# Windowed attention with a gated feed-forward: row maxima and the normalized x turned by VectorE in 32x32 blocks instead of by TensorE

## The chip, the cores and the metric

The kernel runs on one core of a Trainium2 chip. The metric is the device time of one execution in microseconds, the median of the runs. A core has five engines that run side by side: TensorE (PE, with its weight loads as PEld), VectorE (DVE), ScalarE (ACT), GpSimd (POOL) and SyncE (SP, which issues most DMAs).

## What is computed

x is 2048 rows of 512 numbers in float32. Cut to what matters:

```
xn = layernorm(x)                                  # over the 512 columns
q, k, v = split(xn @ wqkv)                         # 32 heads of 16
p = softmax(mask(q @ k.T / 4))                     # a row sees itself and the 255 rows before it
s = (p @ v) @ wo
f = (silu(xn @ w_gate) * (xn @ w_up)) @ w_down     # 1792 hidden columns
out = x + s * silu(f)
```

## The kernel before

**Numbers in two parts.** The large products run on TensorE in a reduced float32 format; every operand is split into a high part (`xh`, `wh`, `hh`) and the difference that is left (`xl`, `wl`, `hl`), and three products are added. The copy of the high part is made by ScalarE, the difference mostly by GpSimd, some of it by VectorE.

**Two halves.** The 128 rows of TensorE's array are used as two halves of 64 (`half(0)`, `half(1)`), each with a queue of matmuls of its own. A result is summed by half 0 first and then by half 1 in the same bank of PSUM; between the two stands a small VectorE copy of one column of that bank (`handover`, L608, tile `ho`), for which half 1 waits.

**Stages.** The 2048 rows are four chunks of 512. For each chunk `load_x` (L252) loads four tiles `xt` of 128 rows, takes mean and variance (VectorE) and scales the tiles (VectorE and GpSimd). `xt_turn` (L621) turns x so that its columns lie on the partitions: for each of four blocks `k` of 128 columns, eight TensorE transposes of 64x64 (four in each half) into two PSUM banks `xp`, then a ScalarE copy to `xh` and a VectorE difference to `xl`. Chunk 0 has a path of its own for the values (`x_turn`, L444), and goes through `xt_turn` as well. The turned x feeds the projections `a` (q and k), `vp` (v), `g` and `u` (gate and up); `d` is the down product and `s` the product with `wo`.

**Attention units.** There are 32 units, eight per chunk, of four heads each. `max_pair` (L1327) computes scores `b` of 128 queries and up to 384 keys; `ttr` (L1345) on VectorE adds the mask and takes the row maximum into a column of the tile `m` (16 columns a unit, one per head and block of queries). When all 16 are there, `max_turn` (L1368) turns `m` by TensorE: a transpose in half 0 into a bank `mt`, a handover copy by VectorE, a transpose in half 1, then a negating copy by ScalarE (`ms`) and a DMA of 8 KB (`put`) that lays the negated maxima as one more row under q. The scores are then computed again as `c`, this time with that row, so that the exponential on ScalarE (`p`) needs no further subtraction; GpSimd cuts the masked corners, and `pv_visit` (L1508) multiplies with the values, in both halves together.

**What sets the order.** A planner in the kernel writes all queues while the program is built. It keeps a clock for each half of TensorE and a queue for VectorE, ScalarE, GpSimd and the DMAs (`do`, L119; `dma`, L128), with a planned cost for each step. The dense matmuls form one long list; the attention steps (`streams`) and the loads (`marks`) have due times in units of 17.6 us of dense work (`PACE`), shifted by `LEAD`. A DMA counts as landed 3.5 us (`LAND`) plus `GUARD` after its issue. At run time every engine takes its instructions in the planned order and waits on semaphores for what it needs.

Of the kernel before, what the change touches and what calls it, by code (L numbers as in the profile page):

```python
# [17 lines left out]
P = 128  # L18
# [29 lines left out]
LAG = 7  # L48
MW = 80
SURE = 0.3  # L50
VDUE = 0.75


# [1 line left out]
PRIO = -0.5  # L55
MM = 0.2315
PACE = 17.6
LEAD = 1.12
OUT = 2.4
STEP = 0.05  # L60
LAND = 3.5
GUARD = 1.5


@with_exitstack
def tile_window_attention_swiglu_gate(
# [128 lines left out]

    ident = pers.tile([P, P], F32, name="ident")
    maskb = pers.tile([P, 3 * P], F32, name="maskb")
    mts = [pers.tile([P, MW], F32, name=f"m{i}") for i in range(2)]
# [11 lines left out]
    def constants2():  # L210
        one = take("one")
        nc.gpsimd.memset(one, 1.0)
        nc.gpsimd.memset(maskb, 0.0)
        nc.gpsimd.affine_select(
            maskb, maskb, [[-1, 3 * P]], ALU.is_ge, NEG, base=2 * P, channel_multiplier=1
        )
        nc.gpsimd.affine_select(
            maskb, maskb, [[1, 3 * P]], ALU.is_gt, NEG, base=0, channel_multiplier=-1
        )
        for t in mts:  # L220
            nc.gpsimd.memset(t, 0.0)
# [12 lines left out]
        nc.gpsimd.memset(vt[:, :, : H * VW].rearrange("p t (h c) -> p t h c", c=VW)[:, :, :, DH], 1.0)  # L234
        nc.gpsimd.memset(vt[:, :, H * VW :], 1.0)
# [16 lines left out]
    def load_x(c):  # L252
# [273 lines left out]
    def w_fetch(j):  # L526
# [18 lines left out]
        for n, (r, u) in enumerate(parts):  # L545
            last = n == len(parts) - 1
            dma(now[0], lambda r=r, u=u, last=last: go(r, u, last),
                lambda t, last=last: w_split(j, t, box[0]) if last else None,
                slack=1.0, can=lambda: box or rfree)

    def w_split(j, t, raw):
        w = [weighted[i].shape[1] if i in weighted else 0 for i in (j, j - 1)]
# [68 lines left out]
    def xt_turn(c, k):  # L621
        left = [2]
        for r in range(2):
# [28 lines left out]

            for t in range(4):
                extra[r].append((128, lambda t=t, go=go: go(t), finished if t == 3 else None))

    PAIRS = ((0, 0), (0, 1), (1, 0))

# [640 lines left out]
    def load_qk(u):  # L1298
# [17 lines left out]

        def then(t, n):
            if n == len(parts) - 1:
                qk_at[u] = t + 1.0
# [7 lines left out]
    def max_pair(u, p, qb):  # L1327
# [6 lines left out]
        for h in range(2):  # L1334
# [24 lines left out]
    mtp = {}  # L1359

    def turn_ready(u, r):
        if r == 0:
            if len(ttr_at.get(u, [])) < 16:
                return None
            return latest([max(ttr_at[u]) + 0.4, bank_time(rb_free)])
        return mtp[u][2]

    def max_turn(u, r):  # L1368
        if r == 0:
            mtp[u] = [*bank(rb_free, f"mt{u}"), None]  # L1370
        pb, tag, _ = mtp[u]

        def go():
            nc.tensor.matmul(
                pb[:MW, R * r : R * r + R], mts[u % 2][half(r), :], ident[half(r), half(r)],
                is_transpose=True, start=True, stop=True,
            )

        if r == 0:
            def after(t):  # L1380
                mtp[u][2] = t

            extra[0].append((128, go, lambda t: do("V", t, 0.09, lambda: handover(pb), after, -1.0)))
            return
        box = []

        def neg():
            box.append(sb(f"ms{u}", [16, P], F32R, "ms", 2))
            nc.scalar.activation(box[0], pb[:16, :P], AF.Copy, scale=-1.0)

        def after_neg(t):
            rb_free[tag] = t
            dma(t, put, lambda t: ms_at.__setitem__(u, t), -3.0, 8)

        def put():
            move(qs[u % 3][48 : 113 : 64], box[0])

        extra[1].append((128, go, lambda t: do("S", t, 0.25, neg, after_neg, -1.0)))

# [199 lines left out]
    def plan_attention():  # L1599
        for u in range(NU):  # L1600
# [2 lines left out]
                marks.append((u - 1 + 0.3, load_qk, (u,)))  # L1603
            for n in range(8):
                streams[0].append((u + 0.02 + 0.1 * n, max_ready, max_pair, (u, n // 4, n % 4)))
            streams[0].append((u + 0.8, turn_ready, max_turn, (u, 0)))
            streams[0].append((u + 0.8, turn_ready, max_turn, (u, 1)))
            ne = 3
            for n in range(2 * ne):
                streams[1].append((u + 1.07 + 0.13 * n, prob_ready, prob_pair, (u, n // 2, n % 2)))  # L1610
# [269 lines left out]
```

## Time and profile before

| | us |
|---|---|
| median of 3 runs | 849.04 (848.96 to 849.66) |
| the profiled execution | 856.25 |
| its span, first to last instruction | 854.5 |
| busy: PE / PEld | 846.9 / 759.8 |
| busy: DVE / ACT / POOL | 503.0 / 489.5 / 627.8 |

The granted TensorE clock is 0.991 of full speed over the span. A row of a group reads: line, engine, operation, output tile <- inputs, shapes, count | busy us, mean ns of one | idle us of the engine just before them, and what ended most of it. A row of waits reads: who waited, for whom, total us, times, longest. A row of the timeline reads: start us, length us, engine, line, operation, and in brackets the idle time before it.

### The profile page before, as it was taken

Reading aid. Unit: us, or ns where it says so; the run is one execution under the profiler, and the core shown is the slowest. Engines: PE = TensorE matmul, PEld = TensorE weight load, DVE = VectorE, ACT = ScalarE, POOL = GpSimd, SP = SyncE. Lnnn points to the kernel's source line nnn. Section 1 sums busy time; section 2 is a strip of 40 time slices with the busy share of each in tenths; the row PEclk is TensorE's granted clock in tenths of the full one; section 3 lists DMA queues with packets and bytes.
Section 4 is the critical chain, followed back from the end, with each engine's and each line's share of the span. In section 5 each row is a group of like instructions: output and inputs, shape, how many; then the busy total and the mean of one; then the engine's idle time right before and its main releaser. Section 6 shows DMA issues by size and latency. Waiting matters only on the chain.

```text
span 854.5 us, 26324 instructions
## 1 busy us (share of the span) xinstructions
PE 846.9 (99%) x10026; PEld 759.8 (89%) x10026; DVE 503.0 (59%) x1676; ACT 489.5 (57%) x950; POOL 627.8 (73%) x887
## 2 busy tenths in 40 slices
PE   8999999999999999999999999999999999999997
PEld 7999988888888989999889888888898899888987
DVE  5238476656666575666657666665646675554235
ACT  5543755556666456565666556656566665565531
POOL 5465877679768598668887687767687976888761
PEclk7999999999999999999999999999999999999999
DMA  5477865767776894578776876674877478754351
GB/s 141 125 203 165 223 151 151 175 155 179 153 191 159 228 226 112 127 197 163 182 164 141 239 187 178 142 183 118 195 184 199 117 169 206 178 136 122 101 140 51
DMA packets 67143, 139.98 MB, mean 164 GB/s; under 512 B 14710, under 2 KB 17654, under 8 KB 67016
## 3 DMA queue, kind: packets, MB, share of 16 engines
q1 hardware_dynamic: 66552, 137.64, 66.3%
q8 instruction: 79, 1.29, 0.7%
q10 hardware_dynamic: 464, 0.66, 0.3%
q14 instruction: 48, 0.39, 0.2%
HBM read 107.68 MB, written 29.62 MB: 161 GB/s over the span
## 4 chain that ended last, share of the span: by engine, by line
PE 98%; DMA 1%; DVE 0%; issue 0%; ACTq 0%; DVEq 0%
PE u L612 19%; PE d L612 19%; PE g L612 19%; PE a L612 11%; PE pv L1536 8%; PE vp L612 6%; PE c L1488 6%; PE s L612 5%; PE b L1340 4%; PE xp L632 1%; DMA xt<-x 1%; PE xp L450 0%; DVE xt L352 0%; DVE s L1189 0%; DVE st L347 0%
## 5 line engine op out<-in xcount | busy, mean ns | idle before, releaser
L572 POOL TENSOR_TENSOR wl<-wr,wh 128x512 fp32r<-128x512 f32 (+1 forms) x239 | 304.8, 1288 | 79.5 <-ACT wh L567 70.9
L1348 DVE CUSTOM_DVE_ANT_0 jk<-b,maskb 128x384 bf16<-128x384 f32 (+2 forms) x512 | 271.4, 530 | 91.2 <-PE b L1340 44.8
L1448 ACT ACTIVATE p<-c 128x512 f32<-128x512 f32 (+2 forms) x384 | 196.2, 573 | 61.7 <-PE c L1488 60.0
L612 PE MATMUL d<-wh,hh 64*128 64x512 f32 x896 | 227.6, 393 | 0.0
L567 ACT ACTIVATE wh<-wr 128x512 fp32r<-128x512 f32 (+1 forms) x239 | 145.8, 629 | 48.0 <-PE s L612 11.6
L612 PE MATMUL g<-xh,wl 64*128 64x512 f32 x448 | 161.3, 394 | 0.0
L612 PE MATMUL u<-xh,wh 64*128 64x512 f32 x448 | 160.8, 393 | 0.0
L612 PE MATMUL g<-xl,wh 64*128 64x512 f32 x448 | 160.6, 394 | 0.0
L612 PE MATMUL g<-xh,wh 64*128 64x512 f32 x448 | 160.3, 393 | 0.0
L612 PE MATMUL u<-xl,wh 64*128 64x512 f32 x448 | 160.2, 394 | 0.0
L612 PE MATMUL u<-xh,wl 64*128 64x512 f32 x448 | 159.8, 393 | 0.0
L612 PE MATMUL d<-wl,hh 64*128 64x512 f32 x448 | 152.7, 394 | 0.0
L612 PEld LDWEIGHTS d<-wh,hh 64*128 64x128 f32 x896 | 140.5, 185 | 6.7
L1460 POOL TENSOR_SCALAR_AFFINE_SELECT p<-p 128x256 f32<-128x256 f32 x256 | 101.6, 409 | 32.1 <-ACT p L1448 30.9
L767 POOL TENSOR_TENSOR hh<-h,hh 128x512 fp32r<-128x512 f32 x56 | 72.5, 1295 | 57.5 <-ACT hh L763 50.6
L1340 PE MATMUL b<-k,q 48*128 48x384 f32 (+2 forms) x512 | 110.6, 331 | 0.0
L1464 POOL TENSOR_SCALAR_AFFINE_SELECT p<-p 128x256 f32<-128x256 f32 x224 | 91.2, 410 | 15.6 <-ACT p L1448 14.1
L1488 PE MATMUL c<-q,k 49*128 49x128 f32 (+2 forms) x704 | 97.6, 299 | 0.0
L612 PE MATMUL a<-xl,wh 64*128 64x512 f32 x256 | 92.9, 392 | 0.0
L612 PE MATMUL a<-xh,wl 64*128 64x512 f32 x256 | 92.7, 392 | 0.0
L612 PE MATMUL a<-xh,wh 64*128 64x512 f32 x256 | 92.3, 392 | 0.0
L1488 PEld LDWEIGHTS c<-q,k 49*128 49x128 f32 x704 | 84.8, 186 | 6.5 <-DVE m L1348 1.1
(118 smaller groups left out, 1903.6 us busy)
## 6 DMA issues: line engine op xcount, KB each, us to landing
wr<-wgu SPq DMA_DIRECT2D x112, 256.0 KB
wr<-wdn SPq DMA_DIRECT2D x48, 256.0 KB
k<-qkd SPq DMA_DIRECT2D x48, 192.0 KB
wr<-wqk SPq DMA_DIRECT2D x32, 256.0 KB
qkd<-qkh SPq DMA_DIRECT2D x32, 256.0 KB
qkd<-qkl SPq DMA_DIRECT2D x32, 256.0 KB
q<-qkd SPq DMA_DIRECT2D x64, 128.0 KB
od<-ev SPq DMA_DIRECT2D x32, 256.0 KB
```

The source lines that it names most:

```text
L567: nc.scalar.activation(wtile[j, h][0][pr, a - 512 * h : b - 512 * h], raw[pr, a:b], AF.Copy)
L572: nc.gpsimd.tensor_tensor(lo, raw[pr, a:b], f32(hi), op=ALU.subtract)
L612: return nc.tensor.matmul(pb, a, b, start=first, stop=last, skip_group_check=True)
L632: nc.tensor.matmul(pb[:, R * t : R * t + R], xt[c, t][half(r), k * P : (k + 1) * P], ident[half(r), half(r)], is_transpose=True, start=Tru ...
L767: nc.gpsimd.tensor_tensor(hl[:, 1, :], self.h, f32(hl[:, 0, :]), op=ALU.subtract)
L1340: nc.tensor.matmul(pb[:, :n], qs[u % 3][r : r + 48, p, qb * P : (qb + 1) * P], ks[u % 3][r : r + 48, p, lo : lo + n], start=True, stop=True,)
L1348: nc.vector.tensor_tensor_reduce(junk[:, :n], pb[:, :n], maskb[:, 3 * P - n :], 1.0, -3.0e38, ALU.add, ALU.max, m[:, col : col + 1],)
L1448: nc.scalar.activation(t[:, h, :], pc[:, :n], AF.Exp, scale=DH ** -0.5)
L1460: nc.gpsimd.affine_select(s, s, [[0, 2], [1, P]], ALU.is_ge, 0.0, base=0, channel_multiplier=-1)
L1464: nc.gpsimd.affine_select(s, s, [[0, 2], [-1, P]], ALU.is_gt, 0.0, base=0, channel_multiplier=1)
L1488: nc.tensor.matmul(pc[:, at0 : at0 + w], ks[u % 3][r : r + 49, p, k0 : k0 + P], qs[u % 3][r : r + 49, p, qb * P : qb * P + w], start=(i == ...
L1536: nc.tensor.matmul(pbs[r][0][32 * j : 32 * j + 32, q0:q1], vt[half(r), (4 * c + kb) % VT, VW * (4 * g + j) : VW * (4 * g + j) + 32], t[hal ...
```

## The change

1. *Row maxima.* `max_turn` and its two entries per unit in the stream are gone. In their place VectorE runs `max_rows` as soon as a unit's 16 maxima are there: it negates the 16 columns into a tile `mn` of 128x32 (the other 16 columns stay zero) and turns it by four 32x32 transposes, one for each group of 32 partitions, into `ms`. The DMA `put` then takes the first 16 rows of `ms`.
2. *x of chunks 1 to 3.* `xt_turn` runs for chunk 0 alone. For the others `x_blocks` is called for each of the four tiles when it is scaled. VectorE turns the tile in four groups of four transposes (32 partitions x 128 elements each, that is four 32x32 blocks) into a tile `xb`; ScalarE then copies the high part (128x512) and GpSimd takes the difference. The groups have a low rank in VectorE's queue until 3.3 units before the chunk begins (`XDD`), a high one after that.
3. *x loaded sooner.* The loads are due 5.847 units before the chunk instead of 5.0.
4. *Constants of the planner:* `LEAD` 1.12 to 1.032, `GUARD` 1.5 to 1.346, and the margin after the loads of q and k from 1.0 to 1.115.

```diff
-LEAD = 1.12
+LEAD = 1.032
-GUARD = 1.5
+GUARD = 1.346
+LXD = 5.847
+XDS = 1.0
+XDD = 3.3
+XDU = 1.5
+QKG = 1.115
...
         def scaled(t, i):
-            normed[c, i] = t
+            x_blocks(c, i, t)
...
+    def x_blocks(c, t, at):
+        xb = []
+        left = [4]
+        tok = slice(t * P, t * P + P)
+        hi, lo = (xn[c % 2][s][:, :, tok] for s in range(2))
+
+        def urgent(n):
+            return lambda: now[0] + 0.1 * t + n * 0.01 + (XDS if work[0] / PACE - LEAD < 8 * c - XDD else -XDU)
+
+        def blocks(b):
+            if not xb:
+                xb.append(take(f"xb{c}_{t}"))
+            q = slice(32 * b, 32 * b + 32)
+            src = xt[c, t][q].rearrange("q (k f d) -> q f k d", f=4, d=32)
+            for f in range(4):
+                dst = xb[0][32 * f : 32 * f + 32].rearrange("d (k b q) -> d b k q", b=4, q=32)[:, b]
+                nc.vector.transpose(dst, src[:, f])
+
+        def turned(at):
+            left[0] -= 1
+            if left[0] == 0:
+                timer(at, lambda: give(xt.pop((c, t))))
+                do("S", at, 0.52, high, lambda at: do("G", at, 1.24, low, ready, XSL), XSL, lambda: c in x_free)
...
+        def high():
+            nc.scalar.activation(hi, view(), AF.Copy)
+
+        def low():
+            nc.gpsimd.tensor_tensor(lo, view(), f32(hi), op=ALU.subtract)
+            timer(free_at["G"] + SURE, give, xb[0])
...
+        for b in range(4):
+            do("V", at, 0.8, lambda b=b: blocks(b), turned, urgent(b), lambda b=b: xb or room(1 + SPARE)())
...
-                ttr_at[u] = ttr_at.get(u, []) + [t]
+                ttr_at[u] = ttr_at.get(u, 0) + 1
+                if ttr_at[u] == 16:
+                    do("V", t, 0.45, lambda: max_rows(u), lambda t: dma(t, lambda: put(u), lambda t: landed(t), -3.0, 8), -1.0)
...
-    def max_turn(u, r):
...
+    def max_rows(u):
+        nc.vector.tensor_scalar(mn[:, :16], mts[u % 2][:, :16], -1.0, None, op0=ALU.mult)
+        rows_of[u] = sb(f"ms{u}", [32, P], F32, "ms", 2)
+        for b in range(4):
+            w = slice(32 * b, 32 * b + 32)
+            nc.vector.transpose(rows_of[u][:, w], f32(mn[w]))
...
-            streams[0].append((u + 0.8, turn_ready, max_turn, (u, 0)))
-            streams[0].append((u + 0.8, turn_ready, max_turn, (u, 1)))
...
-                marks.append((8 * c - 5.0, load_x, (c,)))
-            for k in range(KC):
-                due = 8 * c - 3.5 + 0.25 * k if c else -9.0
-                streams[2].append((due, xt_ready, xt_turn, (c, k)))
+                marks.append((8 * c - LXD, load_x, (c,)))
+            for k in range(KC if not c else 0):
+                streams[2].append((-9.0, xt_ready, xt_turn, (c, k)))
```

What the change moves in the queues, at three places. All lie in unit 20, in the third chunk's feed-forward, where the x of the last chunk is turned. The names: `g2_5` and `g2_6` are gate products, `d2_0_0` to `d2_0_3` down products, `b20` and `c20` the two passes over the scores of unit 20, `jk20` the maxima over them.

PE before, where the maxima of unit 20 are turned (`mt20`), between the gate product of half 1 and the down product of half 0:

```order
L612 MATMUL g2_5_9425<-xh0_79,wl72_0_9233 128x512
L1374 MATMUL mt20_9582<-ident_68,m0_70 80x64
L612 MATMUL d2_0_0_9562<-wh72_1_9256,hh2_1_8321 128x512
L612 MATMUL g2_5_9425<-xh0_79,wh72_0_9232 128x512
L612 MATMUL d2_0_0_9562<-wl72_1_9257,hh2_1_8321 128x512
L612 MATMUL g2_5_9425<-xl0_80,wh72_0_9232 128x512
L612 MATMUL d2_0_0_9562<-wh72_1_9256,hh2_1_8321 128x512
L612 MATMUL g2_5_9425<-xh0_79,wl72_0_9233 128x512
L612 MATMUL d2_0_0_9562<-wh73_0_9267,hh2_2_8866 128x512
L1374 MATMUL mt20_9582<-ident_68,m0_70 80x64
L612 MATMUL g2_5_9425<-xh0_79,wh72_0_9232 128x512
```

PE of the change at the same two products:

```order
L622 MATMUL g2_5_9537<-xh0_80,wl72_0_9337 128x512
L622 MATMUL d2_0_0_9695<-wl72_1_9352,hh2_1_8355 128x512
L1393 MATMUL b21_1_1_9713<-k0_76,q0_73 128x384
L622 MATMUL g2_5_9537<-xh0_80,wh72_0_9336 128x512
L1393 MATMUL b21_1_0_9712<-k0_76,q0_73 128x384
L622 MATMUL d2_0_0_9695<-wh72_1_9351,hh2_1_8355 128x512
L622 MATMUL g2_5_9537<-xl0_81,wh72_0_9336 128x512
L622 MATMUL d2_0_0_9695<-wh73_0_9397,hh2_2_8934 128x512
L622 MATMUL g2_5_9537<-xh0_80,wl72_0_9337 128x512
L622 MATMUL d2_0_0_9695<-wl73_0_9398,hh2_2_8934 128x512
L622 MATMUL u2_5_9644<-xh0_80,wh72_1_9351 128x512
```

The two turns `mt20` are gone, and scores of unit 21 stand where the dense work of unit 20's turn stood.

PE before, where the last block of x of chunk 3 is turned:

```order
L612 MATMUL g2_6_9820<-xh0_79,wl74_0_9548 128x512
L612 MATMUL d2_0_1_9678<-wh74_0_9547,hh2_2_8866 128x512
L632 MATMUL xp3_3_0_9832<-ident_68,xt3_0_8736 128x64
L632 MATMUL xp3_3_1_9833<-ident_68,xt3_0_8736 128x64
L632 MATMUL xp3_3_0_9832<-ident_68,xt3_1_8761 128x64
L632 MATMUL xp3_3_1_9833<-ident_68,xt3_1_8761 128x64
L632 MATMUL xp3_3_0_9832<-ident_68,xt3_2_8770 128x64
L632 MATMUL xp3_3_1_9833<-ident_68,xt3_2_8770 128x64
L632 MATMUL xp3_3_0_9832<-ident_68,xt3_3_8778 128x64
L632 MATMUL xp3_3_1_9833<-ident_68,xt3_3_8778 128x64
L612 MATMUL g2_6_9820<-xh0_79,wh74_0_9547 128x512
L612 MATMUL d2_0_2_9715<-wh73_0_9267,hh2_0_7895 128x512
```

PE of the change, between the end of `d2_0_1` and the start of `d2_0_2`:

```order
L622 MATMUL d2_0_1_9740<-wh74_0_9462,hh2_2_8934 128x512
L622 MATMUL d2_0_3_9845<-wh73_0_9397,hh2_2_8934 128x512
L622 MATMUL d2_0_1_9740<-wl74_0_9463,hh2_2_8934 128x512
L622 MATMUL g2_6_9894<-xh0_80,wh74_0_9462 128x512
L622 MATMUL d2_0_1_9740<-wh74_0_9462,hh2_2_8934 128x512
L1393 MATMUL b21_0_2_9898<-k0_76,q0_73 128x384
L1393 MATMUL b21_0_3_9899<-k0_76,q0_73 128x384
L622 MATMUL g2_6_9894<-xl0_81,wh74_0_9462 128x512
L622 MATMUL d2_0_2_9793<-wh73_0_9397,hh2_0_7925 128x512
```

The eight turns `xp3_3` are gone; gate and down products and the scores follow on each other.

DVE before, from the last maximum of unit 20 on:

```order
L1348 ISA jk20_3_3_9555,m0_70<-b20_3_3_9526,maskb_69 128x384
L1348 ISA m0_70 128x1
L759 SCALAR_TENSOR_TENSOR h2_4_9482<-h2_4_9482,u2_4_9358 128x512
L609 COPY ho_9584<-u2_5_9497 80x1
L609 COPY ho_9592<-mt20_9582 80x1
L647 TENSOR_TENSOR xl1_82<-xp3_1_0_9571,xh1_81 128x4x64
L647 TENSOR_TENSOR xl1_82<-xp3_1_1_9572,xh1_81 128x4x64
L609 COPY ho_9681<-d2_0_0_9562 80x1
```

DVE of the change, from the last but one maximum of unit 20 on:

```order
L1401 ISA jk20_3_3_9554,m0_70<-b20_3_3_9512,maskb_69 128x384
L1401 ISA m0_70 128x1
L1401 ISA jk20_3_2_9569,m0_70<-b20_3_2_9511,maskb_69 128x384
L1401 ISA m0_70 128x1
L682 STREAM_TRANSPOSE xb3_2_9578<-xt3_2_8372 32x4x32 x4
L1420 TENSOR_SCALAR mn_72<-m0_70 128x16
L1424 STREAM_TRANSPOSE ms20_9636<-mn_72 32x32 x4
L802 SCALAR_TENSOR_TENSOR h2_4_9573<-h2_4_9573,g2_4_9384 128x512
L619 COPY ho_9655<-g2_5_9537 80x1
L682 STREAM_TRANSPOSE xb3_2_9578<-xt3_2_8372 32x4x32 x8
L1586 TENSOR_TENSOR ev19_9648<-ev19_9648,pv19_1_9586 128x512
L812 SCALAR_TENSOR_TENSOR h2_4_9573<-h2_4_9573,u2_4_9465 128x512
```

The handover of `mt20` and the differences `xl1` out of PSUM are gone; a group of four turns of x stands ahead of `max_rows` (`mn` and four turns `ms20`), and two groups (x8) stand between a handover and the sum `ev19`.

More of the change, by code (lines that the diff above doesn't have):

```diff
@@ L50 @@
 SURE = 0.3
+CO = 1.07
+MSG = 0.0
+QKG = 1.115
+LXD = 5.847
+XSL = 0.5
+XDS = 1.0
+XDD = 3.3
+XDU = 1.5
+XTD = 3.5
+WSL = 1.0
 VDUE = 0.75
@@ L197, in tile_window_attention_swiglu_gate @@
     maskb = pers.tile([P, 3 * P], F32, name="maskb")
-    mts = [pers.tile([P, MW], F32, name=f"m{i}") for i in range(2)]
+    mts = [pers.tile([P, 32], F32, name=f"m{i}") for i in range(2)]
+    mn = pers.tile([P, 32], F32R, name="mn")
     qs = [pers.tile([P, 2, TC], F32R, name=f"q{i}") for i in range(3)]
@@ L219, in constants2 @@
         )
-        for t in mts:
-            nc.gpsimd.memset(t, 0.0)
+        nc.gpsimd.memset(f32(mn), 0.0)
         def ones(t):
@@ L548, in w_fetch @@
                 lambda t, last=last: w_split(j, t, box[0]) if last else None,
-                slack=1.0, can=lambda: box or rfree)
+                slack=WSL, can=lambda: box or rfree)
     def w_split(j, t, raw):
@@ L1318, in then @@
             if n == len(parts) - 1:
-                qk_at[u] = t + 1.0
+                qk_at[u] = t + QKG
         for n, (a, b) in enumerate(parts):
@@ L1354, in after, with landed, put @@
                 rb_free[tag] = t
-                ttr_at[u] = ttr_at.get(u, []) + [t]
-            extra[h].append((n, go, lambda t, ttr=ttr, after=after: do("V", t, 0.23 + 0.00098 * n, ttr, after, 0.0)))
[L1359 to L1366, printed above, removed]
-    def max_turn(u, r):
[L1369 to L1398, printed above, removed]
+                ttr_at[u] = ttr_at.get(u, 0) + 1
+                if ttr_at[u] == 16:
+                    do("V", t, 0.45, lambda: max_rows(u), lambda t: dma(t, lambda: put(u), lambda t: landed(t), -3.0, 8), -1.0)
+            def landed(t):
+                ms_at[u] = t
+            extra[h].append((n, go, lambda t, ttr=ttr, after=after: do("V", t, 0.23 + 0.00098 * n, ttr, after, 0.0)))
+    rows_of = {}
+    def max_rows(u):
[4 more added lines that the diff above has]
+            nc.vector.transpose(rows_of[u][:, w], f32(mn[w]))
+    def put(u):
+        move(qs[u % 3][48 : 113 : 64], rows_of.pop(u)[:16])
     def pieces(c, e):
```

9 lines of the change are left out of this document (8 added, 1 removed).

## The prediction

> **What bounds the kernel now.** First the page: the span, the busy time of each engine and the chain of work that ended last.
>
> ```profile
> span 854.5 us, 26324 instructions
> PE 846.9 (99%) x10026; PEld 759.8 (89%) x10026; DVE 503.0 (59%) x1676; ACT 489.5 (57%) x950; POOL 627.8 (73%) x887
> ...
> PE 98%; DMA 1%; DVE 0%; issue 0%; ACTq 0%; DVEq 0%
> PE u L612 19%; PE d L612 19%; PE g L612 19%; PE a L612 11%; PE pv L1536 8%; PE vp L612 6%; PE c L1488 6%; PE s L612 5%; PE b L1340 4%; PE xp L632 1%; DMA xt<-x 1%; PE xp L450 0%; DVE xt L352 0%; DVE s L1189 0%; DVE st L347 0%
> ```
>
> The chain is TensorE from end to end: no other engine has 2% of it. Whether TensorE is really fed is not told by its busy share, so next the view of waits, for PE alone: all three rows there are.
>
> ```profile
> PE xp L450 <- DVE xt L352: 1.7, 1, 1.7
> PE warm L250 <- DVE warm L245: 1.1, 1, 1.1
> PE s L612 <- DVE ho L609: 0.4, 1, 0.4
> ```
>
> Two are at the start, one at the end. The groups of weight loads (PEld) show the rest, in the idle time behind the bar:
>
> ```profile
> L1488 PEld LDWEIGHTS c<-q,k 49*128 49x128 f32 x704 | 84.8, 186 | 6.5 <-DVE m L1348 1.1
> L1340 PEld LDWEIGHTS b<-k,q 48*128 48x128 f32 x512 | 71.0, 184 | 7.4 <-issue 0.4 <-DVE m L1348 0.3 <-PE g L612 0.2
> L1536 PEld LDWEIGHTS pv<-p,v 64*32 64x32 f32 x2816 | 50.2, 106 | 29.5 <-issue 9.3 <-ACT ms L1389 0.7 <-ACT wh L567 0.4
> ```
>
> VectorE holds TensorE up by some 1.1 + 0.3 us at the scores and 0.4 us at the end. So the kernel is the sum of what stands in TensorE's two queues (the upper and the lower 64 rows of the array, which run side by side), and an instruction taken out of a queue shortens the span by the time it held that queue, if nothing new makes TensorE wait.
>
> **The change part by part: TensorE.** The order has 160 matmuls fewer: 64 `mt` (two per unit, one in each half) and 96 of the 128 turns of x in `xt_turn` (chunks 1 to 3: 12 groups of eight, four in each half). Chunk 0 keeps its 32.
>
> ```profile
> L1374 PE MATMUL mt<-ident,m 64*80 64x64 f32 x64 | 13.8, 216 | 0.0
> L632 PE MATMUL xp<-ident,xt 64*128 64x64 f32 x128 | 8.3, 224 | 0.0
> ```
>
> A mean of 216 or 224 ns is a latency, not the time that the queue loses. That is read from the timeline of PE around one turn of the maxima and around one group of x (start, us, then the instruction):
>
> ```profile
> 445.08 0.39 PE L612 MATMUL d<-wh,hh 64*128 64x512 f32 x1
> 445.31 0.21 PE L1374 MATMUL mt<-ident,m 64*80 64x64 f32 x1
> 445.33 0.47 PE L612 MATMUL d<-wl,hh 64*128 64x512 f32 x1
> 445.65 0.39 PE L612 MATMUL d<-wh,hh 64*128 64x512 f32 x1
> 445.88 0.39 PE L612 MATMUL d<-wh,hh 64*128 64x512 f32 x1
> ...
> 531.82 0.39 PE L612 MATMUL d<-wh,hh 64*128 64x512 f32 x1
> 532.05 0.41 PE L632 MATMUL xp<-ident,xt 64*128 64x64 f32 x6
> 532.27 0.47 PE L612 MATMUL d<-wh,hh 64*128 64x512 f32 x1
> 532.28 0.28 PE L632 MATMUL xp<-ident,xt 64*128 64x64 f32 x2
> 532.59 0.39 PE L612 MATMUL d<-wl,hh 64*128 64x512 f32 x1
> ```
>
> Undisturbed, `d` follows `d` in 0.23 us (445.65 to 445.88). With `mt` between, two steps take 0.57 us (445.08 to 445.65) instead of 0.46: one `mt` costs its half 0.11 us. With the four turns of x, two steps take 0.77 us (531.82 to 532.59): one group costs a half 0.31 us. Per half 32 x 0.11 + 12 x 0.31 = 3.5 + 3.7 = 7.2 us, the same in both, so the span loses 7.2 us. The bounds: at the rate of the large matmul (0.23 us for 512 columns) the 80 turns of 64 columns in a half would cost 2.3 us; by the mean durations, as if nothing overlapped, 32 x 0.216 + 48 x 0.224 = 17.7 us. I take 7.2, since the timeline shows the queue itself.
>
> **VectorE.** Added: 192 turns of 32 partitions x 128 elements (x, in 48 groups of four), 128 turns of 32 x 32 and 32 small negations (one group of 1 + 4 per unit). Gone: 24 differences for x and 32 handovers of `mt`. No turn is in this trace. The nearest rows, with the two that go:
>
> ```profile
> L704 DVE TENSOR_TENSOR qkl<-a,qkh 128x512 fp32r<-128x512 f32 x32 | 22.0, 688 | 11.7 <-ACT qkh L700 11.3 <-issue 0.4
> L647 DVE TENSOR_TENSOR xl<-xp,xh 128x256 fp32r<-128x256 f32 x32 | 12.4, 416 | 4.7 <-ACT xh L650 4.7
> L609 DVE COPY ho<-mt 80x1 f32<-80x1 f32 x32 | 4.8, 151 | 9.2 <-PE mt L1374 3.1 <-PE u L612 2.1 <-PE a L612 1.2
> ```
>
> From 256 to 512 elements a row grows by 0.272 us, 1.06 ns an element on 0.144 us. An estimate from that line: 0.28 us for 128 elements, 0.178 for 32, 0.161 for 16. That is 192 x 0.28 + 128 x 0.178 + 32 x 0.161 = 82 us, less 24 x 0.416 + 32 x 0.151 = 15 us: VectorE goes from 503 to about 570 us, 67% of the span. All of it lies beside TensorE unless a bank of PSUM or a handover comes late by it. If a turn cost a 256-element row, 0.416, the added work would be 138 us and VectorE at 73%, still not the bound.
>
> What counts is lateness against the plan, since the order is fixed beforehand: the planner gives four turns of x 0.8 us and `max_rows` 0.45. Consecutive VectorE instructions overlap a little in this trace:
>
> ```profile
> 463.28 0.70 DVE L974 TENSOR_TENSOR d<-gp,d 128x512 f32<-128x512 f32 x1 [0.74 <-PE d L612]
> 463.89 0.55 DVE L1348 CUSTOM_DVE_ANT_0 jk<-b,maskb 128x384 bf16<-128x384 f32 x1
> ...
> 467.45 0.15 DVE L609 COPY ho<-a 80x1 f32<-80x1 f32 x1
> 467.53 0.54 DVE L1348 CUSTOM_DVE_ANT_0 jk<-b,maskb 128x384 bf16<-128x384 f32 x1
> ```
>
> The follower starts 0.08 to 0.09 us before the end. With that overlap four turns take 4 x 0.20 = 0.8 us and `max_rows` 0.08 + 4 x 0.10 = 0.48: on plan, no lateness. Without it they take 4 x 0.28 = 1.12 and 0.161 + 4 x 0.178 = 0.87: late by 0.32 us 48 times and by 0.42 us 32 times, 28.9 us in all. So the cost to TensorE lies between 0 and 28.9 us. I take 1.0 us, near the lower end: with 503 us of work, VectorE costs TensorE under 2 us in the rows above, and most of the lateness will fall into its idle third.
>
> The Trainium skill ("VectorE: DVE Perf Modes", section "Two Vector instructions with no wait between them") speaks against the overlap: it says that an instruction whose input or output starts in another group of 32 partitions than the last read or write is held until all earlier ones have finished. By that rule the turns, which change their group each time, would have no overlap, and the sum would stand at the 28.9 us end of the lateness. The instructions quoted above all work from partition 0 on, so no run here shows the rule yet.
>
> **ScalarE, GpSimd, DMA.** ScalarE loses the negated copies of `mt` and the 24 copies out of PSUM and gets 12 from SBUF; GpSimd gets the 12 differences:
>
> ```profile
> L650 ACT ACTIVATE xh<-xp 128x256 fp32r<-128x256 f32 x32 | 10.5, 391 | 2.6 <-PE xp L632 2.5
> L1389 ACT ACTIVATE ms<-mt 16x128 fp32r<-16x128 f32 x32 | 8.4, 261 | 10.5 <-PE d L612 3.1 <-PE mt L1374 2.2 <-PE b L1340 2.2
> L1270 ACT ACTIVATE xh<-o 128x512 fp32r<-128x512 f32 x16 | 9.4, 631 | 1.2 <-POOL o L1265 1.1
> L1273 POOL TENSOR_TENSOR xl<-o,xh 128x512 fp32r<-128x512 f32 x16 | 20.5, 1300 | 1.0 <-ACT xh L1270 1.0
> ```
>
> ScalarE: -32 x 0.261 - 24 x 0.391 + 12 x 0.631 = -10 us. GpSimd: +12 x 1.30 = +15.6 us, to 75%. Neither is on the chain; I cost both at nothing, covered by the 25% of GpSimd that stays idle and by the many dense matmuls between the turned x and the first projection that reads it (in chunk 3, fourteen items of nine or twelve matmuls in each half stand between the last item of `s1`, which frees the buffer, and `a3_0`). The number of DMAs stays; the 12 loads of x are issued 0.85 of a unit sooner, under the same dense work.
>
> The chain of the maxima gets shorter before its DMA, but the plan also asks for it sooner:
>
> ```profile
> 468.60 0.08 DVE L1348 DVE_READ_ACCUMULATOR2_ANT m<- 128x1 f32 x1
> 470.61 0.27 ACT L1389 ACTIVATE ms<-mt 16x128 fp32r<-16x128 f32 x1 [0.19 <-PE g L612]
> 471.21 0.58 SPq L107 DMA_DIRECT2D q<-ms  x1
> 478.45 0.47 PE L1488 MATMUL c<-q,k 49*128 49x128 f32 x4
> ```
>
> Last maximum to issue is 2.6 us here; with `max_rows` in place of the turn it is about 0.9. In the new order at least 23 dense matmuls in a half and one `pv` visit stand between a unit's last `b` and its first `c` (27 before). 23 x 0.23 is 5.3 us without the visit, and the last two maxima, the turn and the issue take some 1.2 + 0.9 + 0.6 = 2.7 of it, and 1.1 more where a group of turns of x stands ahead, as in unit 20. Cover is left for a landing of 1.5 us plus the visit. How long the landing takes is not shown (here under 7.2 us, 471.21 to 478.45, with no wait for it). I cost it at nothing; should it be a microsecond late in the tightest eight units, that is 8 us lost.
>
> **The sum.** The profiled execution took 856.25 us, 854.5 of it span. 856.25 - 7.2 + 1.0 = 850.05. The median of the runs is 849.04, 0.9916 of the profiled one, so the forecast is 850.05 x 0.9916 = 842.9 us. The likeliest case's own range is 841 to 845.
>
> **The rivals.**
> - *VectorE comes late and TensorE waits for PSUM banks (slower).* Place: the scores `b` and `c`, whose banks `jk` frees, and the handovers `ho`, behind two groups of turns put back to back. For it: `b` and `c` already wait for `m` now and then, and TensorE takes its instructions in order, so a wait of one half stops both. Against it: VectorE's idle third. It decides from 7.1 / 28.9, a quarter of the lateness: beyond that there is no gain. At half of it the time is 849.0 - 7.1 + 14.5 = 856.4 us. By the skill's rule on held instructions this case is open; without it the lateness is nil. Chance 0.13.
> - *More than the turns goes (faster still).* The `mt` of the second half waits for a copy of the first, and `pv` starts only where both halves are there; its weight loads stand idle for 29.5 us, 9.3 of them for nothing visible. If 4 us of that go with the turns and VectorE costs nothing, 849.0 - 7.1 - 4 = 838 us. Chance 0.12.
> - *GpSimd gives it back (no change).* 15.6 us more on the engine with the most work after TensorE; it makes the low halves of the weights. If 46% of it reaches TensorE, the 7.1 us are gone: 849 us, within 847.5 to 850.5. Against it: no row of PE's waits names POOL. Chance 0.06.
> - *The change does not do what it says:* settled, the 160 matmuls are not in the new order.
>
> **How the numbers follow.** Forecast 0.69, rivals 0.13, 0.12, 0.06. From 838 to 846.5 the range takes in the forecast, with a VectorE cost of up to 4.6 us, and the second rival; it leaves out the first and the third, 0.19. A difference of 0.2% (1.7 us) is about what a measurement of this kernel can tell from none. Faster: 0.69 + 0.12 = 0.81. The third rival lies within the bound for the most part: 0.05. Slower: the first and the rest of the third, 0.14.
>
> **What would show it.** Right: PE's busy time some 7 us shorter with the span, no `mt` row, 32 `xp` left, still no row of PE waiting for more than 2 us; VectorE near 570 us with the turns of x at 0.2 to 0.3 us. Wrong: new idle time of PEld at `b`, `c` or the dense groups put down to DVE (first rival) or POOL (third); turns of x at 0.4 us or more; a first `c` of a unit that waits for the DMA `q<-ms`.

## The result, and the profile after

| | before | after |
|---|---|---|
| median, us | 849.07 (848.96 to 849.66) | 870.21 (868.37 to 878.04) |
| ratio | | 1.0265, 95% interval 1.0202 to 1.0328 |
| the profiled execution / its span | 856.25 / 854.5 | 869.6 / 867.5 |

The change is slower by 21 us; the forecast was 842.9 us, in a range from 838 to 846.5. The profiled execution of before ran at a mean granted clock of 0.991 (its first slice stands at 7 tenths), that of after at 0.998, so the medians are compared below and not the two spans. Of the experiments below, one run of true_costs (1515.7 us) and one of maxima_reduce (1656.7 us) are left out of the ratios.

The page of after: span, busy times, chain by engine and by line.

```profile
span 867.5 us, 26234 instructions
PE 844.6 (97%) x9866; PEld 755.6 (87%) x9866; DVE 594.2 (68%) x1972; ACT 485.6 (56%) x906; POOL 643.4 (74%) x898
...
PE 81%; DVE 15%; issue 2%; DMA 1%; SPq 0%; ACT 0%; DVEq 0%
PE d L622 16%; PE u L622 15%; PE g L622 15%; PE a L622 10%; PE pv L1565 7%; DVE xb L682 5%; PE vp L622 5%; PE c L1517 5%; PE s L622 4%; DVE jk L1401 4%; PE b L1393 4%; DVE mn L1420 2%; DVE ms L1424 1%; DVE h L812 1%; DMA xt<-x 1%
```

The chain was PE from end to end; now 15% of it is VectorE, and its three new groups are there by name: the turns of x (`xb`, 5%), the negation (`mn`, 2%) and the turns of the maxima (`ms`, 1%), with the maxima `jk` that stand behind them. PE's waits, three rows before, are fourteen; the first five, and then the two groups of weight loads with their idle time and what ended it:

```profile
PE b L1393 <- DVE m L1401: 3.8, 7, 1.5
PE vp L622 <- DVE ho L619: 2.5, 1, 2.5
PE c L1517 <- DVE m L1401: 2.2, 5, 1.1
PE d L622 <- DVE ho L619: 1.8, 2, 1.1
PE pv L1565 <- DVE m L1401: 1.4, 2, 0.9
...
L1517 PEld LDWEIGHTS c<-q,k 49*128 49x128 f32 x704 | 86.7, 186 | 12.2 <-DVE m L1401 5.8 <-issue 1.9
L1393 PEld LDWEIGHTS b<-k,q 48*128 48x128 f32 x512 | 76.7, 184 | 17.1 <-DVE m L1401 10.7 <-issue 1.2
```

Ahead of the scores the loads stood idle for 6.5 and 7.4 us, 1.4 of it behind VectorE. Now it is 12.2 and 17.1 us, 16.5 of it behind `m`: banks of PSUM that a late maximum had not yet freed. The new VectorE work, by group:

```profile
L682 DVE STREAM_TRANSPOSE xb<-xt 32x128 f32<-32x128 f32 x192 | 58.1, 303 | 3.0
L1424 DVE STREAM_TRANSPOSE ms<-mn 32x32 f32<-32x32 f32 x128 | 25.7, 200 | 2.4
L1420 DVE TENSOR_SCALAR mn<-m 128x16 fp32r<-128x16 f32 x32 | 24.4, 763 | 0.6
```

Two of the means lie a little above the estimate (303 ns against 280, 200 against 178). The third lies far above it: 763 ns against 161 for sixteen elements a row. The view of the tile `mn` gives its spread (shortest/median/longest, ns):

```profile
L1420 DVE TENSOR_SCALAR mn<-m x32: 167/398/5412, 69.2 to 788.1; 128x16 fp32r<-128x16 f32 x32
```

And the timeline of the longest, VectorE first, GpSimd below it:

```profile
209.78 0.08 DVE L1401 DVE_READ_ACCUMULATOR2_ANT m<- 128x1 f32 x1
209.89 5.41 DVE L1420 TENSOR_SCALAR mn<-m 128x16 fp32r<-128x16 f32 x1
215.34 0.84 DVE L1424 STREAM_TRANSPOSE ms<-mn 32x32 f32<-32x32 f32 x4
...
209.89 1.30 POOL L582 TENSOR_TENSOR wl<-wr,wh 128x512 fp32r<-128x512 f32 x1
211.14 0.41 POOL L1489 TENSOR_SCALAR_AFFINE_SELECT p<-p 128x256 f32<-128x256 f32 x1
211.51 2.52 POOL L582 TENSOR_TENSOR wl<-wr,wh 128x512 fp32r<-128x512 f32 x2
213.99 1.28 POOL L1318 TENSOR_TENSOR o<-o,r 128x512 f32<-128x512 f32 x1
```

A 0.17 us instruction lasts 5.41 us, from 209.89 to 215.30, and GpSimd works without a gap over the same time: its `o` ends at 213.99 + 1.28 = 215.27. Each GpSimd instruction begins some 0.05 us before the one ahead of it has ended. The 20 negations that last longer than 0.2 us all end 0.03 to 0.04 us after a GpSimd instruction ends. What such a wait does to TensorE shows at the second longest:

```profile
641.08 3.80 DVE L1420 TENSOR_SCALAR mn<-m 128x16 fp32r<-128x16 f32 x1
644.92 0.84 DVE L1424 STREAM_TRANSPOSE ms<-mn 32x32 f32<-32x32 f32 x4
645.70 0.10 DVE L619 COPY ho<-vp 80x1 f32<-80x1 f32 x1
```

The handover `ho` of `vp` stands behind the negation and the turns. It is the 2.5 us wait in the list above: neither half of TensorE runs a matmul from 643.33 to 645.85.

The turns show the other half of the lateness, in a row of VectorE's timeline for one group of x:

```profile
500.18 1.25 DVE L682 STREAM_TRANSPOSE xb<-xt 32x128 f32<-32x128 f32 x4
```

Four turns of 0.303 us take 1.25 us, where the plan has 0.8: no overlap at all between them. The four turns of the maxima take 0.84 us (215.34 above). So against its plan VectorE is late by 48 x (1.25 - 0.8) = 21.6 us with x, and by 32 x (0.763 + 0.84 - 0.45) = 36.9 us with the maxima, 58.5 us in all.

### The profile page after: what moved, and what is told of

The parts are those of the page before. It is cut to its first block, busy times and chain, and to the rows that moved or that the text cites. A ratio compares the mean times of both kernels' runs of the same rounds, so it can differ in the third digit from the quotient of the medians.

```text
span 867.5 us, 26234 instructions
## 1 busy us (share of the span) xinstructions
PE 844.6 (97%) x9866; PEld 755.6 (87%) x9866; DVE 594.2 (68%) x1972; ACT 485.6 (56%) x906; POOL 643.4 (74%) x898
## 3 DMA queue, kind: packets, MB, share of 16 engines
q8 instruction: 78, 1.28, 0.7%
## 4 chain that ended last, share of the span: by engine, by line
PE 81%; DVE 15%; issue 2%; DMA 1%; SPq 0%; ACT 0%; DVEq 0%
PE d L622 16%; PE u L622 15%; PE g L622 15%; PE a L622 10%; PE pv L1565 7%; DVE xb L682 5%; PE vp L622 5%; PE c L1517 5%; PE s L622 4%; DVE jk L1401 4%; PE b L1393 4%; DVE mn L1420 2%; DVE ms L1424 1%; DVE h L812 1%; DMA xt<-x 1%
## 5 line engine op out<-in xcount | busy, mean ns | idle before, releaser
L622 PE MATMUL d<-wh,hh 64*128 64x512 f32 x896 | 229.3, 394 | 2.5 <-DVE ho L619 1.8
L622 PE MATMUL u<-xh,wh 64*128 64x512 f32 x448 | 166.8, 394 | 0.4 <-DVE ho L619 0.4
L622 PE MATMUL u<-xh,wl 64*128 64x512 f32 x448 | 165.8, 393 | 0.0
L622 PE MATMUL u<-xl,wh 64*128 64x512 f32 x448 | 165.7, 394 | 0.0
L622 PE MATMUL g<-xh,wl 64*128 64x512 f32 x448 | 165.0, 394 | 0.0
L622 PE MATMUL g<-xh,wh 64*128 64x512 f32 x448 | 164.4, 393 | 0.0
L622 PE MATMUL g<-xl,wh 64*128 64x512 f32 x448 | 164.3, 393 | 0.0
L622 PE MATMUL d<-wl,hh 64*128 64x512 f32 x448 | 160.4, 392 | 0.0
L622 PEld LDWEIGHTS d<-wh,hh 64*128 64x128 f32 x896 | 145.0, 185 | 9.3 <-DVE ho L619 2.7
L1393 PE MATMUL b<-k,q 48*128 48x384 f32 (+2 forms) x512 | 120.6, 333 | 4.9 <-DVE m L1401 3.8
L1517 PE MATMUL c<-q,k 49*128 49x128 f32 (+2 forms) x704 | 101.1, 302 | 3.9 <-DVE m L1401 2.2
L1493 POOL TENSOR_SCALAR_AFFINE_SELECT p<-p 128x256 f32<-128x256 f32 x224 | 91.5, 409 | 15.3 <-ACT p L1477 13.6
L1517 PEld LDWEIGHTS c<-q,k 49*128 49x128 f32 x704 | 86.7, 186 | 12.2 <-DVE m L1401 5.8
L622 PE MATMUL a<-xh,wh 64*128 64x512 f32 x256 | 93.8, 392 | 0.0
L622 PE MATMUL a<-xh,wl 64*128 64x512 f32 x256 | 93.4, 391 | 0.0
L622 PE MATMUL a<-xl,wh 64*128 64x512 f32 x256 | 93.2, 391 | 0.0
```

The source lines that it names most:

```text
L622: return nc.tensor.matmul(pb, a, b, start=first, stop=last, skip_group_check=True)
L1393: nc.tensor.matmul(pb[:, :n], qs[u % 3][r : r + 48, p, qb * P : (qb + 1) * P], ks[u % 3][r : r + 48, p, lo : lo + n], start=True, stop=True,)
L1493: nc.gpsimd.affine_select(s, s, [[0, 2], [-1, P]], ALU.is_gt, 0.0, base=0, channel_multiplier=1)
L1517: nc.tensor.matmul(pc[:, at0 : at0 + w], ks[u % 3][r : r + 49, p, k0 : k0 + P], qs[u % 3][r : r + 49, p, qb * P : qb * P + w], start=(i == ...
```

## The experiments

The theory after this reading: the turns of x and the negation's wait for GpSimd each make VectorE late, and TensorE pays for both. The rivals: the loss lies in the constants and the loads, or in the new plan itself. The medians of before beside these runs were 849.1 to 849.5 us; each ratio is against them.

**1. neg_reduce.** The negation by another kind of instruction, the order unchanged:

```diff
-nc.vector.tensor_scalar(mn[:, :16], mts[u % 2][:, :16], -1.0, None, op0=ALU.mult)
+nc.vector.tensor_reduce(mn[:, :16], mts[u % 2][:, :16].unsqueeze(2), mybir.AxisListType.X, ALU.max, negate=True)
```

> The changed kernel with one instruction of each unit replaced: the negation of the 16 maxima (mn) by a reduction over an axis of length one with negated result. Same order on every engine. Theory P (a VectorE tensor_scalar from SBUF to SBUF has to wait until GpSimd is between instructions; 24.4 us for 32 of them, up to 5.4 us for one, holds VectorE and behind it the PSUM banks that TensorE needs): mn falls to 0.2 us each, 19 us of VectorE go, and the time falls from 870 by 10 to 17 us, to 853 to 860 us. Theory X (the turns of x are what is late, 1.26 us for four against 0.8 planned, 22 us in all): the time falls by 5 us or less, to 865 us or more. Theory C (LEAD, GUARD and the other constants make a worse plan): no change, 868 to 872.

Measured: 859.67 us, ratio 1.012 (1.0103 to 1.0137). The group of the negation, by line:

```profile
L1420 DVE TENSOR_REDUCE mn<-m 128x16 fp32r<-128x16 f32 x32 | 5.3, 167 | 0.6
```

From 763 to 167 ns, and 10.5 us of the time gone: theory P, at the upper end of its range. The weight loads ahead of `c` and `b` still stand idle for 6.0 + 10.4 = 16.4 us behind `m`, as in the changed kernel, so that idle time comes with the turns of x. What went are waits for handovers: PE's rows of waits for `ho` sum to 5.7 us in the changed kernel and to 1.0 here. The Trainium skill ("SBUF — State Buffer", section "Who interferes with whom") says that VectorE and GpSimd share a pair of ports, which the one that issues first holds for its whole instruction, that `tensor_scalar` can need the pair and that on trn2 `tensor_reduce` never does. The 763 and 167 ns agree with that; that one wait can reach over several GpSimd instructions (5.41 us above) is what this trace adds.

**2. x_quick and 3. both_quick.** The four turns of a group become one of 128x128, in the second together with the negation of experiment 1. This leaves out the exchange of blocks between the groups of 32 partitions, so the turned x is not the right one. It also takes some 45 us of work off VectorE (58.1 to 13.2 us for the turns), not the lateness alone.

```diff
-            for f in range(4):
-                dst = xb[0][32 * f : 32 * f + 32].rearrange("d (k b q) -> d b k q", b=4, q=32)[:, b]
-                nc.vector.transpose(dst, src[:, f])
+            nc.vector.transpose(xb[0][:, P * b : P * b + P], xt[c, t][:, P * b : P * b + P])
```

> The changed kernel with each group of four turns of x replaced by a single one over 128 partitions, which leaves out the exchange of blocks between the groups of 32 partitions; same order otherwise, the negation mn as in the changed kernel. A group takes about 0.32 us instead of 1.26, so it is early against its planned 0.8 us. Theory X: the time falls from 870 by 12 us or more, to 858 or less. Theory P: the waits of mn remain, the time falls by 5 us or less. If both matter: 855 to 865.

> Both replacements at once (the exchange of blocks left out, the negation by a reduction), same order. If the lateness of VectorE is all that went wrong, the gain that was forecast appears: 841 to 846 us. If the constants of the planner or anything else of the plan costs time, it stays above 850.

Measured: x_quick 854.68 us, ratio 1.0085 (1.0049 to 1.0122); both_quick 842.2 us, ratio 0.9917 (0.9903 to 0.9932). x_quick lies where theory X has it, but its ten runs spread from 851.4 to 862.9 us, over two of the three forecasts. both_quick shows that these two are all that went wrong: without them the time is what the prediction had summed, 842.2 against 842.9 us. The slow turns of x are worth 870.2 - 854.7 = 15.5 us or 859.7 - 842.2 = 17.5 us, the slow negation 10.5 or 12.5 us. The intervals of the changed kernel and of x_quick reach some 5 and 3 us to either side, so the 2 us between these pairs mean nothing. PE's waits in both_quick but the last row (0.3 us), its two groups of weight loads, and one row of VectorE's timeline:

```profile
PE c L1517 <- DVE m L1401: 1.1, 1, 1.1
PE warm L260 <- DVE warm L255: 1.1, 1, 1.1
PE xp L460 <- DVE xt L362: 1.0, 1, 1.0
...
L1517 PEld LDWEIGHTS c<-q,k 49*128 49x128 f32 x704 | 85.5, 186 | 6.8 <-DVE m L1401 1.7
L1393 PEld LDWEIGHTS b<-k,q 48*128 48x128 f32 x512 | 76.0, 184 | 7.2 <-DVE m L1401 1.5
...
95.86 0.68 DVE L678 STREAM_TRANSPOSE xb<-xt 128x128 f32<-128x128 f32 x3
```

The idle time at the scores is back at 6.8 and 7.2 us. And three turns on all 128 partitions, 0.294 us each on the mean, take 0.68 us: they start 0.19 us apart and overlap by a third. The turns that change their group of 32 partitions (0.303 us each, four in 1.25) do not overlap.

**4. constants.** Before, with the three constants of the change alone:

```diff
-LEAD = 1.12
+LEAD = 1.032
...
-GUARD = 1.5
+GUARD = 1.346
...
-                qk_at[u] = t + 1.0
+                qk_at[u] = t + 1.115
```

> The kernel before with the three constants of the change alone (LEAD 1.032, GUARD 1.346, the margin after the loads of q and k 1.115); the maxima and x are turned by TensorE. Theory C: slower than before by 5 us or more. Theories P and X: 847 to 851 us, as before.

Measured: 850.85 us, ratio 1.0036 (1.0014 to 1.0058). They cost 1.6 us by themselves (1.2 to 4.9 by the interval); theory C does not hold. The parts then add up: 849.3 + 1.6 - 7.2 + 17 (x) + 10.5 (negation) = 871 us. The last two terms were taken from differences to this very kernel, so the sum tests the first three alone: 843.7 us, against the 842.2 of both_quick. both_quick has the sooner loads of x as well, so no loss lies in them.

**5. true_costs.** The negation of experiment 1, and a plan that knows how long the steps take:

```diff
-            do("V", at, 0.8, lambda b=b: blocks(b), ...
+            do("V", at, 1.2, lambda b=b: blocks(b), ...
...
-                    do("V", t, 0.45, lambda: max_rows(u), ...
+                    do("V", t, 0.85, lambda: max_rows(u), ...
```

> The changed kernel with the negation by a reduction and with the planner told what was measured: 1.2 us (and its 0.14 us of latency) for four turns of x instead of 0.8, 0.85 for the turn of the maxima instead of 0.45. The plan is another one; the work is the same. If lateness against the plan is the cause, not the load of VectorE as such: from 859.7 to 842 to 848 us. If VectorE simply has too much to do at these places: 855 us or more.

Measured: 852.95 us, ratio 1.0034 (1.0013 to 1.0055). This is between the two forecasts: most of the waits for `m` are gone (past its start no row of PE's waits sums to more than 0.5 us, and the weight loads ahead of `c` and `b` stand 5.2 us behind `m`, against 16.4 in neg_reduce and 3.2 in both_quick), and 6.7 us with them, but 10.7 us more than both_quick are left. The plan now gives the turns their time: in the first turned chunk the last turn of x begins at 163.3 us, in both_quick at 139.9 (7.4 of the 23.4 us are a lower clock at the start of this profiled execution).

Where the 10.7 us go can be read by the times of the 5760 dense matmuls (L622), which both kernels have. Past the start true_costs falls behind both_quick by some 2 us up to 230 us, by 5 to 6 us between 230 and 405, and by 3 to 4 after that; the steepest parts lie in or just behind the second and third stretch of turns (297 to 354 and 490 to 550 us). VectorE is busy for 87 to 89% of the three stretches, in both_quick for 67 to 69%. So the loss lies where VectorE is fullest; by which step it reaches TensorE is not shown.

**6. maxima_reduce, 7. maxima_true_costs, 8. x_alone, 9. maxima_tensor_scalar.** The two halves of the change by themselves. In 6 and 7 x stays with TensorE, the constants are those of before, and the negation is that of experiment 1; 7 also plans `max_rows` at 0.85. In 9 the negation is the `tensor_scalar` of the change. In 8 the maxima stay with TensorE and all else is the change.

> The kernel before with the maxima alone turned by VectorE, the negation by a reduction; x by TensorE, all constants as before. The 64 turns mt are worth 3.5 us by the queue time read before; VectorE is late by some 0.45 us per unit. 845 to 847 us if that lateness costs nothing, 849 or more if it takes the gain.

> As the run before it, with 0.85 us planned for the turn of the maxima instead of 0.45. If the lateness of the maxima costs TensorE time: 1 to 3 us less than that run. If not: the same within 1 us, 845 to 847.

> The changed kernel with the maxima turned by TensorE as before; x by VectorE, planned at 0.8 us for a group that takes 1.26, constants as changed. The turns of x give TensorE 3.7 us; their lateness cost 17.5 us between the two runs with and without it (859.7 and 842.2). If the two parts add up: 849.3 + 1.6 (constants) - 3.7 + 17.5 less what the turn of the maxima adds to it, 858 to 866 us. If x alone is harmless and only the pile of both is not: 850 us or less.

> The kernel before with the maxima alone turned by VectorE, as in the change: the negation is the tensor_scalar, the constants are those of before, x stays with TensorE. It differs from maxima_reduce (847.7 us) by that one instruction per unit. Theory A (the tensor_scalar waits for the port that GpSimd holds, 0.6 us a unit on the mean, and that lateness reaches TensorE): the negation again takes 0.5 to 1.2 us on the mean and the time is 855 to 859 us, the 10.5 us of neg_reduce. Rival B (the wait only hurts together with the turns of x): within 2 us of maxima_reduce.

Measured: maxima_reduce 847.73 us, ratio 0.9968 (0.9948 to 0.9987); maxima_true_costs 846.11, ratio 0.9954 (0.9935 to 0.9972); x_alone 860.17, ratio 1.0127 (1.007 to 1.0185); maxima_tensor_scalar 860.49, ratio 1.0128 (1.0093 to 1.0164). maxima_reduce lies between its two forecasts; planning the true cost saves 1.6 us more, as forecast; x_alone is in its range. So the maxima by VectorE are worth 1.7 us, and 3.4 us where the plan knows their cost, and these two are the versions of the whole computation that beat both kernels. In 9 one instruction per unit of the wrong kind makes the kernel 12.8 us slower than maxima_reduce: theory A, above its range of 855 to 859 us, with a negation of 1.36 us on the mean, above the 0.5 to 1.2 that were expected. Rival B does not hold: the wait hurts without the turns of x. The tile `mn` in maxima_tensor_scalar, and PE's longest wait there:

```profile
L1367 DVE TENSOR_SCALAR mn<-m x32: 167/550/7730, 67.1 to 780.7; 128x16 fp32r<-128x16 f32 x32
...
PE u L612 <- DVE ho L609: 7.5, 3, 5.0
```

One negation lasts 7.73 us. The wait of 5.0 us for a handover `ho` lies behind another one, of 5.55 us (298.55 to 304.10; the handover begins at 304.91). x alone costs 11 us by the side of before, and its loads ahead of `b` stand idle for 13.3 us, 7.9 of it behind `m`.

**10. single_turns, 11. single_turns_before_const.** true_costs with each turn of x as a step of its own (planned at 0.32 us) in place of groups of four, in 11 with the three constants of before:

```diff
-        for b in range(4):
-            do("V", at, 1.2, lambda b=b: blocks(b), turned, urgent(b), ...
+        for b, f in ((b, f) for b in range(4) for f in range(4)):
+            do("V", at, 0.32, lambda b=b, f=f: blocks(b, f), turned, urgent(b + f / 4), ...
```

> As true_costs (negation by a reduction, max_rows planned at 0.85 us), but each turn of x is a step of its own in VectorE's queue, planned at 0.32 us, instead of a group of four planned at 1.2. Theory A (what is left in true_costs is blocking: a group of four, 1.25 us, or two of them, 2.5 us, stands ahead of maxima and handovers): the time falls by at least half of the 10 us between true_costs and the runs with quick turns, to 843 to 848 us. Rival B (the sum of VectorE's work in the stretches where x is turned is what costs, however it is cut): 851 to 854 us, as true_costs.

> As single_turns, with LEAD, GUARD and the margin after the loads of q and k as in the kernel before. Theory A (the constants cost 1.6 us here as they do alone, by the experiment constants): 1.6 us below single_turns. Rival B (the constants were chosen for the turned x and help with it): at or above single_turns.

Measured: 890.23 us, ratio 1.0483 (1.0465 to 1.0501), and 889.04, ratio 1.0469 (1.0453 to 1.0484). Both theories of single_turns are wrong: finer steps are 37 us slower. The line of the granted clock on its page, in tenths of full speed for 40 slices, and below it the table of windows of 5 us at the first fall (us; busy PE, PEld, DVE, ACT, POOL, each with its instructions; granted clock, DMA share, GB/s):

```profile
PEclk9999999979999999789999999969999999999999
...
165.00:170.00 5.00, 5.00 (x78) 3.59 (x81) 4.56 (x20) 1.91 (x4) 2.77 (x4) 1.00 0.53 136
170.00:175.00 5.00, 3.35 (x38) 1.93 (x18) 4.67 (x15) 3.05 (x6) 3.17 (x6) 0.89 0.45 130
175.00:180.00 5.00, 4.76 (x14) 3.33 (x15) 2.24 (x12) 2.57 (x7) 4.94 (x10) 0.50 0.99 205
180.00:185.00 5.00, 5.00 (x14) 3.83 (x13) 0.15 (x1) 0.63 (x1) 1.27 (x1) 0.50 0.04 7
185.00:190.00 5.00, 5.00 (x35) 4.01 (x36) 0.67 (x3) 0.74 (x2) 1.30 (x1) 0.74 0.01 3
190.00:195.00 5.00, 5.00 (x58) 4.25 (x62) 4.14 (x17) 3.02 (x6) 2.10 (x3) 1.00 0.59 158
```

The clock falls three times. At the first, the border of the second chunk, PE has no dense product between the last `d` (168.08) and the first `a` (177.69), since the turned x comes too late; GpSimd's `xl` there, and PE's first product that reads it:

```profile
176.87 1.27 POOL L696 TENSOR_TENSOR xl<-xb,xh 128x512 fp32r<-128x512 f32 x1
...
178.20 0.79 PE L622 MATMUL a<-xl,wh 64*128 64x512 f32 x1
```

`xl` ends at 178.14 and the product starts at 178.20. Until then TensorE lives on a few scores (in windows of 1 us it is busy for 2.6 of the 4 us from 170 to 174); its clock falls to half at 173.9 and stays there to 187.6, for some 13.6 us. An estimate from the mean granted clock of 0.971: the falls alone are worth 0.029 x 887 = 26 of the 37 us. Experiment 11 adds nothing to the question of the constants: 1.2 us apart, within the spread of each.

**12. true_costs_early.** true_costs with x loaded still sooner (`LXD` 7.2).

> As true_costs (852.95 us), with x loaded 7.2 units before its chunk instead of 5.847; in the order the last turn of x of each chunk then stands up to a unit sooner among the maxima (unit 4 instead of 5, 12 instead of 13). Theory A (the 10 us that true_costs stands above the kernel with short turns come from x that is finished too near to the chunk that needs it, in the longer stretch that the turns take at their true length): at least half of it goes, 843 to 848 us, and the second and third chunk begin as soon as before. Rival B (the turns cost wherever VectorE does them, since each group stands for 1.25 us ahead of maxima and handovers): 851 us or more, with the loss moved to the units where the turns stand now.

Measured: 865.6 us, ratio 1.0199 (1.0182 to 1.0216). Theory A does not hold. Rival B does by its words (851 us or more, the loss where the turns stand now), but it did not foresee the size: the time is 12.7 us above true_costs. The windows of 4 us at the place, in the same columns:

```profile
276.00:280.00 4.00, 3.90 (x22) 2.88 (x20) 3.71 (x13) 2.81 (x6) 2.25 (x6) 1.00 0.67 227
280.00:284.00 4.00, 2.89 (x10) 1.66 (x12) 3.52 (x12) 2.21 (x4) 3.83 (x7) 0.67 0.69 225
284.00:288.00 4.00, 4.00 (x13) 3.10 (x12) 3.65 (x15) 1.08 (x2) 1.32 (x3) 0.50 0.52 195
288.00:292.00 4.00, 4.00 (x11) 2.84 (x9) 3.10 (x12) 0.00 (x0) 0.00 (x0) 0.50 0.78 270
292.00:296.00 4.00, 4.00 (x99) 2.04 (x98) 0.11 (x1) 0.00 (x0) 0.00 (x0) 0.62 0.03 10
...
279.26 1.26 DVE L682 STREAM_TRANSPOSE xb<-xt 32x128 f32<-32x128 f32 x4
```

A group of turns stands ahead of the maxima at 279.26, scores wait, TensorE is thin from 280 us on (busy for 2.89 of 4 us), and the clock is at half from 281.3 to 295.0. The clock falls at one earlier place as well (0.84 from 90 to 100 us). An estimate from the mean granted clock, 0.987 against the 0.999 or so of true_costs past its start: 0.012 x 863 = 10 of the 12.7 us. Moving the turns moved the loss, and the falls of the clock made it larger.

## Why the prediction was wrong

- **TensorE, -7.2 us: right as far as the runs can tell.** both_quick lies 7.1 us under before. That this is within 0.1 us is in part luck, since both_quick also carries the constants, 1.6 us by themselves. The maxima alone, 32 x 0.11 = 3.5 us in the sum, gave 3.4 (maxima_true_costs).
- **VectorE's durations: near for the turns, wrong for the negation.** The turns took 303 and 200 ns against 280 and 178, the negation 763 against 161. The negation was priced from a line through `tensor_tensor` rows, another kind of instruction. Rows of before already showed that a `tensor_scalar` can be long here:

```profile
L352 DVE TENSOR_SCALAR xt<-xt,mv 128x512 f32<-128x512 f32 x1 | 1.5, 1532 | 0.0
L372 DVE TENSOR_SCALAR hv<-mv 128x4 f32<-128x4 f32 x1 | 1.1, 1093 | 0.0
L371 DVE TENSOR_SCALAR warm<-mv 128x4 f32<-128x4 f32 x1 | 0.2, 154 | 0.0
```

  Four elements a row in 1093 ns at one place and in 154 at another. The nearest row by kind would have bounded the negations at 32 x 1.093 = 35 us.
- **The lateness: the step that failed.** It was bounded at 0 and 28.9 us and taken at 1.0 "near the lower end", on an overlap read from instructions that all begin at partition 0. The upper end was the right one for the turns: x late by 0.45 us a group (0.32 was its bound), the maxima's four turns 0.84 us (4 x 0.178 = 0.71 was theirs). The lateness was 21.6 + 36.9 = 58.5 us, twice the upper end: of the 29.6 us between them the negation has 32 x (0.763 - 0.161) = 19.3 and the longer turns the rest. Of the 58.5 us 870.2 - (849.1 + 1.6 - 7.2) = 27 us reached TensorE, a little under half. Not all of the 27 are lateness against the plan: with the negation fast and the true prices planned, 10.7 us are left (true_costs), so the sentence that all of VectorE's work "lies beside TensorE" did not hold either. The Trainium skill ("VectorE: DVE Perf Modes", section "Two Vector instructions with no wait between them") says that an instruction that starts in another group of 32 partitions is held until all earlier ones have finished. The traces agree: 1.25 us for four turns that change their group, 0.68 us for three that do not.
- **"Most of the lateness will fall into its idle third": too hopeful.** A little over half of it did (31 of 58.5 us), where the sum let all but 1.0 us fall there. The plan puts the turns where the maxima and handovers are dense; a late VectorE there is waited for at once, in both halves (643.33 to 645.85 us above).
- **The first rival is what happened,** in place and mechanism (`b`, `c` and the handovers behind VectorE); its price, half of 28.9, was too low because the lateness was 58.5 us; two thirds of what lies above 28.9 is the negation's. Its chance, 0.13, was too small, since the only rows against it were of instructions that do not change their group.
- **GpSimd: the sum was right (643.4 us against 643 expected), the place was not.** No row of PE's waits names POOL, as expected. GpSimd costs time through VectorE, whose negation waits for it, and not by the 15.6 us of added work: in maxima_tensor_scalar, without that work, the negation waits longer (1.36 us on the mean).
- **ScalarE and the DMA:** ScalarE 3.9 us less instead of 10, off the chain either way. A wait for `q<-ms` stands in the traces of neg_reduce (1.4 us), x_quick (2.2) and true_costs (0.2), against a bound of 8.
- **The constants** had no price in the sum; they cost 1.6 us (1.2 to 4.9).
- **Open:** why x costs more than its planned price in true_costs. Shown are the later end of the turns and the places of the loss, in the stretches where VectorE is busy for 87 to 89%; that the chunk needs the turns there is shown for single_turns alone, and no plan was found in which x by VectorE gains.

## What to carry to other kernels

Before work is moved to an engine with idle time, price it by a row of the same kind of instruction and the same partitions, and ask what stands behind it in that engine's queue: with a third of the time idle, 58 us of lateness still cost 27. Where VectorE and GpSimd run side by side, a small `tensor_scalar` on a chain that matters can be a `tensor_reduce` with a negated output, for 167 ns instead of 763. In true_costs a plan that knows the price avoided most of the waits but not the cost, and where a plan thinned TensorE's work for some microseconds (single_turns, true_costs_early) the clock fell as well.

## What the runs showed of the hardware

- A VectorE `tensor_scalar` of 128x16 waits for GpSimd over several instructions in a row, not for one: 5.41 us (after) and 7.73 us (maxima_tensor_scalar) against 0.167.
- Turns of 32 partitions that change their group follow each other after their whole length (four of 0.303 us in 1.25), turns of 128 partitions after 0.19 us of 0.294 (three in 0.68, both_quick).
- The granted clock fell to 0.50 without a long gap. In single_turns, by windows of 1 us, it fell at 173.9 us, after some 4 us in which PE was busy for 2.6, with no gap of more than 0.44 us in PE's timeline. In true_costs_early it fell at 281.3, 1.4 us after the first gap, with none of more than 0.66 us. Both times it was back at full 13.6 or 13.7 us after the fall.
